# A third buffer for raw weight blocks, v loaded two to three units later into three buffers, and seven buffers for split factors

## The chip, the cores and the metric

The kernel runs on one core of a Trainium2 chip. The metric is the device time of one execution in microseconds. The profile is of one further execution; its times are in us from the start of its span.

## What is computed

Three stages follow one another: a local attention over chunks of 32 queries, a first gated layer (w1, w2, w3 and w_out of `moe`), and a second gated layer (w_a, w_b and w_out of `moe2`).

```python
# attention: q, k, v (4, 8, 768, 64), 8 memory rows; chunk 32, 16 to the left, 8 to the right
scores = scale * q_c @ concat(mem_k, k_ctx).T          # per chunk and head
a = exp(scores - max); a = a / (sum(a) + 1e-9)
out = a @ concat(mem_v, v_ctx)
# first layer, x (3072, 512)
x = ((x @ w1) * (x @ w2) @ w3) @ w_out                  # d_ff 1024
# second layer
y = ((x @ w_a) * (x @ w_b)) @ w_out                     # d_ff 1536
```

## The kernel before

The kernel works in float32. A factor of a product is split into a high and a low part in one narrower form, and three matrix multiplies replace one. The weights arrive as 64-bit words, in **raw blocks** of 128 x 512 x 8 bytes (512 KB). A raw block is scaled by two ScalarE instructions in place (`w_scale`, L358 and L359) and put together by three VectorE instructions (`w_bits`, L363 to L365); in what follows these three are "the sum" of the block. After the sum its buffer is free.

**Stage 0** multiplies w3 by w_out (the tiles `wps`, the loop from L562) in two halves of 8 steps k with 4 products m each. **The first layer** (`ti` from 0 to 5, 512 tokens each) makes `psA`, `psB` and `psY`, in 24 half-steps of a dozen multiplies for each `ti`. **The second layer** (from the last `ti` on) uses seven products in place of eight per pair of blocks; its factors are made from w_a and w_b by `c_weights` during the first layer, split into `co` tiles (L139, L142) and stored to DRAM (L470).

The engines run their instructions in the order in which the program issues them, and this order is written out by hand. Three streams are woven together in it:

- **Attention.** There are 64 units u (half of the heads of 96 queries). `attn_slot` runs one slot s; a unit takes three slots. The stages of unit u stand at these slots: scores (TensorE) at 3u, max (VectorE) 3u+1, exp (ScalarE) 3u+2, norm (GpSimd, L217) 3u+3, transposition (TensorE, `pt`) 3u+5, copy of `pt` (ScalarE, L229) 3u+6, product with v (TensorE, `xp`) 3u+7 for an odd u, which takes units u-1 and u together, and the split into `xt` at 3u+8. `a_load` loads k, q and v of a unit on the SyncE queue at slot 3u-4 for u up to 23, and at 3u-7 after that. `kbuf` and `qbuf` have two buffers, `vraw` has six. The program loads k, q and v of unit 1 twice.
- **Weights of stage 0 and the first layer.** `plan` is a list of 40 raw blocks, numbered from 0. `w_tick` is one step: the low part of an older block, the high part of another, the sum of block n, the scaling of block n+1, and then as many loads as there are free buffers. Blocks up to 25 take buffers from two pools in turn (`BUFS["raw64"]` gives their number: 2 in `stage`, 3 in `p0`), later ones from `stage` alone. So a load waits on SyncE for the sum that freed its buffer, and what the program issues on SyncE after it waits too.
- **Weights of the second layer.** `blocks_of` loads the 24 raw blocks of w_a and w_b with the two buffers of `stage`, one load after each sum, two blocks ahead.

Within a slot the program issues the stages first (x, pv, pt, trans, norm, exp, max, scores), then the loads. In stage 0, first half, each k issues one tick and a slot after m = 1, and one tick and two slots after m = 3. In the second half, k below 6, one slot follows m = 1, and one or two ticks and then one or two slots follow m = 3. In the first layer each half-step issues a tick (later one step of `c_weights`) and then one or two slots.

In the last `ti` the attention's pool is closed and `co` moves from two buffers in `stage` to a pool of its own (`cop`, 8 buffers).

Of the kernel before, what the change touches and what calls it, by code (L numbers as in the profile page):

```python
# [7 lines left out]
F32 = mybir.dt.float32  # L8
F32R = mybir.dt.float32r
U32 = mybir.dt.uint32  # L10
# [3 lines left out]
P = 128  # L14
B, H, S, D = 4, 8, 768, 64
# [5 lines left out]
HH = 4  # L21
TT = 512
NT1 = B * S // TT
NU = B * NG * 2
# [6 lines left out]
M2 = DF2 // P  # L31
NEG = -1.0e30
CH = 512
BUFS = {"raw64": (2, 3), "dec": (2, 4)}
W3FB = 8
A0 = (1, 2)
TB = 2
# [7 lines left out]
def tile_attention_moe(  # L45
# [24 lines left out]
    stage = stagestack.enter_context(tc.tile_pool(name="stage", bufs=2))  # L70
# [3 lines left out]
    att = astack.enter_context(tc.tile_pool(name="att", bufs=2, side="right"))  # L74
# [32 lines left out]
    vraw, masked = {}, [None, None]  # L107

    def a_mask(u, eng):
        if u < NPLAIN and masked[u % 2] != kind_of(u):  # L110
            masked[u % 2] = kind_of(u)
            m = mask[0:GQ:CHUNK, kind_of(u), :]
            eng.dma_start(
                out=kbuf[u % 2][D:KA], in_=m[:, None, :].to_broadcast([3, HH, KW])
            )
# [9 lines left out]
        eng.dma_start(out=qbuf[u % 2][0:D], in_=qt[u])  # L125

    def a_v(u):
        v = vraw[u] = att.tile([P, HH * D], F32, tag="vraw", bufs=6, name="vraw")
        nc.sync.dma_start(out=v, in_=vw[u])

    def a_load(u):
        if u >= NU:
            return
        a_mask(u, nc.sync)
        a_qk(u, nc.sync)
        a_v(u)

    def split_hi(hi, src):
        nc.scalar.activation(hi, src, AF.Copy)  # L139
# [145 lines left out]
    def attn_slot(n=1):  # L285
        for _ in range(n):
            s = acount[0]
            if s >= NSLOT:
                return
            acount[0] += 1  # L290
            for off, stage_of in STAGES:
                u, r = divmod(s - off, 3)
                if r == 0 and 0 <= u < NU:
                    stage_of(u)

            if s % 3 == 0 and s // 3 + 1 > NPLAIN + 1:
                a_prep_lo(s // 3 + 1)
            if s % 3 == 2 and s // 3 + 2 > NPLAIN + 1:
                a_prep_hi(s // 3 + 2)
            if s % 3 == 0 and NPLAIN <= s // 3 + 1 <= NPLAIN + 1:  # L300
                a_prep_hi(s // 3 + 1)
            if s % 3 == 1 and NPLAIN <= s // 3 + 1 <= NPLAIN + 1:
                a_prep_lo(s // 3 + 1)
            if s % 3 == 2:
                if s // 3 + 2 <= NPLAIN + 1:
                    a_load(s // 3 + 2)
                if s // 3 + 3 >= NPLAIN + 2:
                    a_load(s // 3 + 3)

# [17 lines left out]
    def w_tile(i, tag, shape):  # L329
        x = 0  # L330
        if i < NW0:

            x = int(turn[tag][1] * BUFS[tag][0] < turn[tag][0] * BUFS[tag][1])
        n = BUFS[tag][x]
        if live[tag][x] == n:
# [95 lines left out]

    def blocks_of(stage, src, out, bufs):

        raws = []

        def load():
            if src:
                r = stage.tile([P, CH, 2], U32, tag="raw64", bufs=2, name="raw64")  # L440
                nc.sync.dma_start(out=r.rearrange("p c w -> p (c w)"), in_=src.pop(0))
                raws.append(r)

        load()
        load()
        yield
        while raws:
            r = raws.pop(0)
            w_scale(r)
            yield  # L450
            a = stage.tile([P, CH], U32, tag="dec", bufs=bufs, name="dec")
            w_bits(a, r)
            load()
            out.append(a.bitcast(F32))
            yield

    def c_weights():
        blocks = []
        conv = blocks_of(stage, [wab[f, :, c] for f in range(M2) for c in range(2)], blocks, 2)

        def halves(items):


            n = CH // 2
            x, hl = {}, {}
            for i in range(len(items) + 1):
                if i > 0:
                    co, hi, lo = hl.pop(i - 1)
                    split_lo(lo, x.pop(i - 1), hi)
                    nc.sync.dma_start(out=items[i - 1][0], in_=co.bitcast(F32))  # L470
                for m in range(i, min(i + 2, len(items))):
                    if m not in x:
                        x[m] = items[m][1]()
                if i < len(items):
                    pool, bufs = co_in[0]
                    co = pool.tile([P, 2, n], F32R, tag="co", bufs=bufs, name="co")
                    hi, lo = co[:, 0, :], co[:, 1, :]
                    if len(x[i].shape) == 3:
                        hi, lo = (v.rearrange("p (k f) -> p k f", k=2) for v in (hi, lo))
                    split_hi(hi, x[i])  # L480
                    hl[i] = co, hi, lo
                yield

        def add(x, y, op):
            z = stage.tile([P, CH // 2], F32, tag="cs", bufs=2, name="cs")
            z = z.rearrange("p (k f) -> p k f", k=2)
            nc.vector.tensor_tensor(z, x, y, op)
            return z

        next(conv)  # L490
        yield
        for f in range(M2):
            blocks.clear()
            for _ in range(4):
                next(conv)
                yield
            h = [b.rearrange("p (k j f) -> p k j f", k=2, j=2) for b in blocks]
            a11, a12, a21, a22 = h[0][:, :, 0], h[1][:, :, 0], h[0][:, :, 1], h[1][:, :, 1]
            last = []

            def sums(x, y, op):
                last[:] = [add(x, y, op)]
                return last[0]

            items = (
                (0, lambda: a11),
                (3, lambda: sums(a21, a22, ALU.add)),
                (2, lambda: sums(last[0], a11, ALU.subtract)),
                (5, lambda: sums(a12, last[0], ALU.subtract)),
                (4, lambda: sums(a11, a21, ALU.subtract)),  # L510
                (1, lambda: a12),
                (6, lambda: a22),
            )
            yield from halves(
                [(wcd[f][:, i, :].rearrange("p (l c) -> p l c", l=2), x) for i, x in items]
            )
    co_in = [(stage, 2)]
# [170 lines left out]
    for ti in range(NT1):  # L688
        last = ti == NT1 - 1
        gs = {}  # L690
        attn_slot(NEED[ti] - acount[0])
        if last:
            astack.close()
            tp = ctx.enter_context(tc.tile_pool(name="tp", bufs=2, side="right"))
            costack = ExitStack()
            cop = costack.enter_context(tc.tile_pool(name="cop", bufs=8, side="right"))
            co_in[0] = cop, 8
            xs = []
        for m in range(M1):
            gs[m] = (d1 if m < 4 else d1b).tile(  # L700
                [P, 2, TT], F32R, tag="g2", bufs=4, name="g2"
            )
            ab_step(w12s[m], xt[ti], gs[m], between)
            if last:
                del w12s[m]
                xs.append(x_new())
                if m == 0:
                    w7_load(0)
                if m == 2:
                    b11, b21 = x_first(xs, 0, ti - 1)  # L710
        for n in (0, 2, 1, 3) if last else range(KD):
            psY = psd.tile([P, 512], F32, tag="d", name="psY")
            i = 0
            for m in range(M1):
                for a, b in PASSES:
                    mm(
                        psY[:, :TT],
                        wsm[m][:, a, P * n : P * n + P],
                        gs[m][:, b, :],
                        i == 0,  # L720
                        i == 3 * M1 - 1,
                    )
                    i += 1
                if m == M1 // 2 - 1:
                    between()
            between()
            psY = psY[:, :TT]
            if not last:
                ys = d1b.tile([P, TT], F32, tag="ys", bufs=1, name="ys")
                nc.scalar.activation(ys, psY, AF.Copy)  # L730
                nc.sync.dma_start(out=yd[ti][:, n, :], in_=ys)
            elif n < 2:
                b12 = tmp()
                nc.scalar.activation(b12, psY, AF.Copy)
                t1 = minus(psY, b11)
                x_put(xs[3], n, t1)
            else:
                late = x_rest(xs, n - 2, b11, b21, b12, t1, psY)
                next(late)
                if n == 2:  # L740
                    for _ in late:
                        pass
                    b11, b21 = x_first(xs, 1, ti - 1)
        if last:
            w7_load(1)
# [252 lines left out]
```

## Time and profile before

| | us |
|---|---|
| median of 3 runs | 1143.05 |
| lowest and highest | 1139.79, 1143.15 |
| profiled execution, its own time | 1140.1 |
| its span | 1138.0 |
| TensorE busy in the span | 1096.9 (96%) |
| VectorE busy | 648.3 (57%) |
| ScalarE busy | 516.1 (45%) |
| GpSimd busy | 286.2 (25%) |

A busy share is a mean over stages with different limits, so the reading starts with windows by stage, and goes on to what TensorE waited for in each. The granted clock of TensorE is given as a share of its higher level. An idle time in front of an instruction stands in square brackets with what ended it; a wait for several things is put down to the one that came last.

### The profile page before, as it was taken

To read this page: it belongs to the slowest core of one execution; us is meant where nothing else is said; L and a number is where in the kernel's file an instruction comes from. 1 tells how busy PE (TensorE), PEld (TensorE's weight loads), DVE (VectorE), ACT (ScalarE), POOL (GpSimd) and SP (SyncE) were. 2 spreads that over 40 slices of the span, in tenths; PEclk is the share of its full clock that TensorE was granted. 3 is DMA by queue.
4 is the path that set the end of the run, shared out by engine and by line. 5 is a ranking of instruction groups with operands and counts; after the bars stand their busy time and mean duration, and the time that the engine had idled before them with its cause. 6 is when DMAs were issued, how large, how long until landed. Compare 5 with 4: busy or idle time off the path is not lost.

```text
span 1138.0 us, 15580 instructions
## 1 busy us (share of the span) xinstructions
PE 1096.9 (96%) x5344; PEld 874.6 (77%) x5344; DVE 648.3 (57%) x1374; ACT 516.1 (45%) x1321; POOL 286.2 (25%) x265
## 2 busy tenths in 40 slices
PE   4997999999999999999999999999999999999998
PEld 2554777887777887887887778888888888888887
DVE  6896866787998887874666554343223234232220
ACT  4776664666676575664444434232222223222210
POOL 1111231232232331331203322302323310223210
PEclk9999999999999999999999999999999999999999
DMA  9854435335445334424554554353433451434311
GB/s 268 244 184 127 150 117 182 127 133 172 144 134 179 129 131 167 154 101 149 212 185 185 206 224 152 136 169 107 188 131 132 183 175 60 181 130 177 147 37 37
DMA packets 65684, 174.91 MB, mean 154 GB/s; under 512 B 8168, under 2 KB 20870, under 8 KB 60998
## 3 DMA queue, kind: packets, MB, share of 16 engines
q1 hardware_dynamic: 54791, 107.58, 28.7%
q0 software_dynamic: 10528, 66.08, 15.6%
q8 instruction: 42, 0.69, 0.3%
q14 instruction: 36, 0.29, 0.1%
q10 hardware_dynamic: 287, 0.27, 0.1%
HBM read 140.33 MB, written 33.55 MB: 153 GB/s over the span
## 4 chain that ended last, share of the span: by engine, by line
PE 74%; DVE 4%; ACT 3%; issue 3%; DMA 2%; POOL 1%; SPq 0%; ACTq 0%; DVEq 0%; POOLq 0%
PE ps L784 29%; PE ops L93 17%; PE psA L93 10%; PE psB L93 9%; PE psY L93 6%; DMA wc<-co 1%; PE sc L93 1%; PE xp L93 1%; ACT t L204 1%; PE pt L225 1%; DVE q L142 1%; DVE dec L365 1%; DVE dec L364 1%; POOL t L217 0%; ACT k L139 0%
## 5 line engine op out<-in xcount | busy, mean ns | idle before, releaser
L784 PE MATMUL ps<-x,w 128*128 128x512 f32 x1512 | 349.5, 389 | 3.2 <-ACT tmp L796 3.2
L784 PEld LDWEIGHTS ps<-x,w 128*128 128x128 f32 x1512 | 283.4, 188 | 63.9 <-ACT tmp L796 5.3
L801 DVE TENSOR_TENSOR tmp<-ps,tmp 128x512 f32<-128x512 f32 x108 | 74.6, 691 | 245.3 <-PE ps L784 241.2
L93 PE MATMUL psA<-xt,w 128*128 128x512 f32 x576 | 145.6, 400 | 3.2 <-ACT xt L139 2.3
L93 PE MATMUL psB<-xt,w 128*128 128x512 f32 x576 | 141.0, 393 | 0.0
L93 PE MATMUL psY<-g,wo 128*128 128x512 f32 x576 | 139.0, 393 | 0.0
L217 POOL TENSOR_TENSOR t<-t,sm 96x512 f32<-96x512 f32 x64 | 81.8, 1278 | 222.2 <-DVE sm L216 126.6
L683 POOL DMA_DIRECT2D w<-wc x72 | 39.4, 551 | 368.4 <-PE ps L784 368.0
L796 ACT ACTIVATE tmp<-ps 128x512 f32<-128x512 f32 x108 | 64.4, 596 | 147.3 <-PE ps L784 109.0
L93 PEld LDWEIGHTS psA<-xt,w 128*128 128x128 f32 x576 | 106.3, 190 | 28.1 <-ACT xt L139 3.5
L93 PEld LDWEIGHTS psY<-g,wo 128*128 128x128 f32 x576 | 105.6, 188 | 21.0
L93 PEld LDWEIGHTS psB<-xt,w 128*128 128x128 f32 x576 | 105.5, 188 | 21.0
L93 PE MATMUL ops<-wo,g 128*128 128x512 f32 x504 | 118.6, 389 | 0.0
L618 POOL TENSOR_TENSOR g<-gv,g 128x512 fp32r<-128x512 f32 x48 | 67.8, 1412 | 189.0 <-ACT g L617 170.6
L93 PEld LDWEIGHTS ops<-wo,g 128*128 128x128 f32 x504 | 94.6, 188 | 19.6
L807 ACT ACTIVATE g<-tmp 128x512 fp32r<-128x512 f32 x66 | 40.8, 633 | 130.2 <-DVE tmp L806 130.2
L808 POOL TENSOR_TENSOR g<-tmp,g 128x512 fp32r<-128x512 f32 x66 | 87.4, 1338 | 26.6 <-ACT g L807 25.7
L93 PE MATMUL wps<-wo_f,w3f 128*128 128x512 f32 x128 | 65.0, 640 | 11.1 <-DVE wo_f L365 10.3
L204 ACT ACTIVATE t<-t,mx 96x128 f32<-96x128 f32 x168 | 65.1, 390 | 13.7 <-DVE mx L189 13.6
L93 PE MATMUL ops<-fo,g 128*128 128x512 f32 x288 | 68.2, 389 | 0.0
L358 ACT ACTIVATE raw<-raw 128x512 f32<-128x512 f32 x76 | 50.9, 670 | 30.5 <-DMA raw<-in_w 18.8
L93 PEld LDWEIGHTS ops<-fo,g 128*128 128x128 f32 x288 | 54.1, 188 | 11.2
(79 smaller groups left out, 1276.0 us busy)
## 6 DMA issues: line engine op xcount, KB each, us to landing
w<-wc POOLq DMA_DIRECT2D x36, 1024.0 KB, 6.6
w<-wc POOLq DMA_DIRECT2D x36, 768.0 KB, 4.7
wc<-co SPq DMA_DIRECT2D x84, 256.0 KB, 2.4
raw<-in_wab SPq DMA_DIRECT2D x24, 512.0 KB, 3.8
kraw<-in_kt SPq DMA_DIRECT2D x42, 256.0 KB, 3.0
vraw<-in_vw SPq DMA_DIRECT2D x65, 128.0 KB, 2.9
raw<-in_w3a SPq DMA_DIRECT2D x16, 512.0 KB, 5.1
raw<-in_w SPq DMA_DIRECT2D x16, 512.0 KB, 3.8
```

Of the source, the lines that this page charges most:

```text
L93: nc.tensor.matmul(o, lhsT=l, rhs=r, start=first, stop=last)
L142: nc.vector.tensor_tensor(lo, src, hi.bitcast(F32), ALU.subtract)
L204: nc.scalar.activation(t[:, h, :], src[:, h, :], AF.Exp, bias=mx[:, h : h + 1], scale=scale, accum_out=sm[:, h : h + 1],)
L217: nc.gpsimd.tensor_tensor(t, t, sm[:, :, None].to_broadcast([GQ, HH, KW]), ALU.mult)
L358: nc.scalar.activation(h, h, AF.Copy, scale=2.0**-112)
L618: nc.gpsimd.tensor_tensor(g2[:, 1, :], gv, g2[:, 0, :].bitcast(F32), ALU.subtract)
L683: nc.gpsimd.dma_start(out=t[:, c0:c1].bitcast(F32), in_=src[:, c0:c1])
L784: nc.tensor.matmul(ps, lhsT=w[:, i, a, k, :], rhs=xs[i][:, b, k, :], start=first and n == 0, stop=n == 5, skip_group_check=not first,)
L796: nc.scalar.activation(z, ps, AF.Copy)
L801: nc.vector.tensor_tensor(z, ps, y, ALU.add)
L807: nc.scalar.activation(g2[:, 0, :], z, AF.Copy)
L808: nc.gpsimd.tensor_tensor(g2[:, 1, :], z, g2[:, 0, :].bitcast(F32), ALU.subtract)
```

## The change

The pool `stage` gets three buffers for raw blocks, for `w_load` and for `blocks_of` in `c_weights` alike. `a_load` no longer loads v; instead a slot s with s mod 3 = 1 and s from 10 on loads v of unit s/3 - 1, that is v of unit u at slot 3u+4, into one of three buffers. `cop` has seven buffers in place of eight.

```diff
-BUFS = {"raw64": (2, 3), "dec": (2, 4)}
+BUFS = {"raw64": (3, 3), "dec": (2, 4)}
     def a_v(u):
-        v = vraw[u] = att.tile([P, HH * D], F32, tag="vraw", bufs=6, name="vraw")
+        if u >= NU:
+            return
+        v = vraw[u] = att.tile([P, HH * D], F32, tag="vraw", bufs=3, name="vraw")
         nc.sync.dma_start(out=v, in_=vw[u])
     def a_load(u):
...
         a_qk(u, nc.sync)
-        a_v(u)
     def attn_slot(n=1):
...
                     a_load(s // 3 + 3)
+            if s % 3 == 1 and s // 3 > 2:
+                a_v(s // 3 - 1)
-    def blocks_of(stage, src, out, bufs):
+    def blocks_of(stage, src, out, bufs, raws_n=2):
...
-                r = stage.tile([P, CH, 2], U32, tag="raw64", bufs=2, name="raw64")
+                r = stage.tile([P, CH, 2], U32, tag="raw64", bufs=raws_n, name="raw64")
     def c_weights():
-        conv = blocks_of(stage, [...], blocks, 2)
+        conv = blocks_of(stage, [...], blocks, 2, 3)
...
-            cop = costack.enter_context(tc.tile_pool(name="cop", bufs=8, side="right"))
-            co_in[0] = cop, 8
+            cop = costack.enter_context(tc.tile_pool(name="cop", bufs=7, side="right"))
+            co_in[0] = cop, 7
```

## Rows read from the trace of the kernel before

**Rows 1.** Windows: length; busy PE, PEld, DVE, ACT, POOL; PEclk; DMA share, GB/s.

```profile
0.00:26.00 26.00, 10.47 (x33) 5.26 (x34) 15.17 (x29) 13.56 (x27) 4.15 (x10) 0.95 0.91 274
26.00:84.00 58.00, 56.18 (x280) 31.12 (x281) 53.54 (x108) 43.78 (x137) 10.81 (x10) 0.96 0.72 211
84.00:108.50 24.50, 18.68 (x81) 9.44 (x76) 14.50 (x28) 12.85 (x36) 2.07 (x2) 0.93 0.51 158
108.50:165.00 56.50, 51.07 (x285) 41.44 (x286) 44.54 (x79) 36.78 (x102) 15.55 (x12) 0.97 0.40 126
...
205.00:599.00 394.00, 390.46 (x2121) 317.60 (x2120) 306.96 (x792) 237.53 (x698) 112.29 (x85) 1.00 0.45 152
```

**Rows 2.** Waits of PE from 84 to 166: us in total, times, longest.

```profile
PE xp L93 <- ACT p L229: 4.3, 2, 2.7
PE pt L225 <- ACT raw L358: 3.1, 1, 3.1
PE pt L225 <- POOL t L217: 2.4, 1, 2.4
```

**Rows 3.** Waits of ACT from 84 to 166.

```profile
ACT raw L358 <- DMA raw<-in_w: 15.4, 10, 2.5
```

**Rows 4.** Timeline of PE from 94: start, us, instructions, [idle before <- releaser].

```profile
94.81 0.68 PE L225 MATMUL pt<-id_sb,t 96*128 96x96 f32 x4 [3.13 <-ACT raw L358]
95.28 3.52 PE L93 MATMUL wps<-wo_f,w3f 128*128 128x512 f32 x4
...
99.51 1.88 PE L93 MATMUL wps<-wo_f,w3f 128*128 128x512 f32 x4
...
103.48 0.55 PE L93 MATMUL xp<-p,vraw 128*64 128x96 f32 x8 [1.61 <-ACT p L229]
...
115.56 2.89 PE L93 MATMUL psA<-xt,w 128*128 128x512 f32 x12
...
125.67 0.80 PE L93 MATMUL xp<-p,vraw 128*64 128x96 f32 x8 [2.73 <-ACT p L229]
...
126.40 4.33 PE L93 MATMUL psA<-xt,w 128*128 128x512 f32 x12
```

**Rows 5.** Timeline of VectorE and ScalarE before the stop at 94.81.

```profile
87.74 0.69 DVE L365 CUSTOM_DVE_ANT_0 dec<-raw,dec 128x1024 uint16<-128x1024 uint16 x1
...
89.90 0.67 ACT L358 ACTIVATE raw<-raw 128x512 f32<-128x512 f32 x1 [2.40 <-DMA raw<-in_w]
```

**Rows 6.** Timeline around the load of k of unit 10.

```profile
69.38 0.47 SPq L124 DMA_DIRECT2D kraw<-in_kt  x1
...
71.97 0.69 DVE L365 CUSTOM_DVE_ANT_0 w3f<-raw,w3f 128x1024 uint16<-128x1024 uint16 x1
...
75.46 1.04 PE L93 MATMUL sc<-kraw,qraw 67*96 67x128 f32 x8
```

**Rows 7.** Timeline around the product with v of units 2 and 3.

```profile
44.50 0.33 SPq L346 DMA_DIRECT2D raw<-in_w3b  x1
44.92 0.47 SPq L124 DMA_DIRECT2D kraw<-in_kt  x1
...
47.96 1.01 PE L93 MATMUL xp<-p,vraw 128*64 128x96 f32 x16
```

**Rows 8.** DMA issues of the whole span: count, KB each, median us to landing.

```profile
vraw<-in_vw SPq DMA_DIRECT2D x65, 128.0 KB, 2.9
...
qraw<-in_qt SPq DMA_DIRECT2D x64, 96.0 KB, 3.9
...
raw<-in_w3b SPq DMA_DIRECT2D x8, 512.0 KB, 4.5
```

**Rows 9.** Timeline of PE: two further waits in stage 0.

```profile
62.00 1.98 PE L93 MATMUL wps<-wo_f,w3f 128*128 128x512 f32 x4 [0.71 <-DVE wo L558]
...
69.76 1.08 PE L93 MATMUL sc<-kraw,qraw 67*96 67x128 f32 x8 [0.80 <-DMA qraw<-in_qt]
```

**Rows 10.** Waits of the SyncE queue: us in total, times, longest.

```profile
SPq L441 <- DVE dec L365: 201.1, 28, 12.5
```

**Rows 11.** Timeline of VectorE beside a GpSimd instruction.

```profile
118.23 1.67 DVE L364 SCALAR_TENSOR_TENSOR dec<-raw,dec 128x512 uint32<-128x512 uint32 x1
```

More of the change, by code (lines that the diff above doesn't have):

```diff
@@ L458, in c_weights @@
         blocks = []
-        conv = blocks_of(stage, [wab[f, :, c] for f in range(M2) for c in range(2)], blocks, 2)
+        conv = blocks_of(stage, [wab[f, :, c] for f in range(M2) for c in range(2)], blocks, 2, 3)
         def halves(items):
```

## Prediction

> **What bounds the kernel now.** I read the windows by stage first. From 205 us to 599 us TensorE is busy 390.46 of 394 us, and the second layer behind it holds only products that the change does not touch, so what can be won or lost lies before 205 us [rows 1]. Three stages differ there. Up to 26 us the DMA engines are 91% busy and TensorE waits for weights. From 26 to 84 us TensorE (56.18 of 58) and VectorE (53.54 of 58) are both nearly full. From 84 to 165 us TensorE is busy 18.68 of 24.5 and 51.07 of 56.5 us: some 11 us are idle, and VectorE has 10 and 12 us to spare [rows 1].
>
> Then the waits of TensorE between 84 and 166 us: 3.1 us once for `pt`, put down to a scaling of a raw block, 4.3 us in two stops for the copy of `pt` that ScalarE makes, and 2.4 us for the norm on GpSimd [rows 2]. What ScalarE itself waits for in the same stretch is ten times a raw block, 15.4 us in all [rows 3]. So TensorE is stopped by exp and copies that stand behind a scaling on ScalarE, and the scaling stands behind a load. The timeline shows why: the sum of a block ends at 88.43 (87.74 + 0.69), only then is its buffer free for another load, while the next scaling already waits for a load of the tick before and starts at 89.90 after 2.40 us of idle time [rows 5]. A w3b block takes 4.5 us from issue to landing in the median [rows 8].
>
> The stops cost more than their length. After the one at 94.81 four multiplies took 3.52 us, and 1.88 us a little later; after the one at 125.67 twelve took 4.33 us against 2.89 before [rows 4]. That is the lower of TensorE's two levels (1.2 against 2.4 GHz, the factor of 1.87) for a while: 1.64 and 1.44 us.
>
> **The change part by part.** The order of the work on TensorE, ScalarE, VectorE and GpSimd is the same; the DMAs move along SyncE and one v load (unit 1, loaded twice) goes. The sum is made against the profiled execution, 1140.1 us, which lies 0.26% below the median of 1143.05.
>
> *Raw blocks, 84 to 165 us.* From block 27 on each load has two ticks to land instead of one. The wait of ScalarE before 94.81 goes. I follow its chain: with 2.40 us out of ScalarE, exp and norm end about 92 us, when TensorE has just finished its multiplies (94.81 less 3.13 is 91.68), so the whole stop and its slow clock go: 3.13 + 1.64 = **4.8 us** (3.1 if the clock falls anyway). At 103.48 the copy of `pt` stands behind a scaling too, but also behind a high part that needs a VectorE sum; I take 0.9 of the 1.61 us (0 to 1.6). At 125.67 the two scalings ahead waited by 1.5 us each in the mean (15.4 / 10), and a high part between them needs VectorE's sum; I take 2.0 of 2.73 us, and the 1.44 us of clock with it: **3.4 us** (1.2 to 4.2). The 2.4 us for the norm come through VectorE, which is late by the same waits; half of it, 1.2 (0 to 2.4).
>
> *Raw blocks, k behind them.* This part costs. SyncE issues in order, so what stands behind a load waits for the sum that this load waits for. Going through the ticks by hand: k of unit 10 stood behind a load that reuses the buffer of block 20; with three buffers a load that reuses the buffer of block 22 comes just ahead of it. That sum ends at 72.66 (71.97 + 0.69), VectorE is 92% busy in this stage [rows 1] and won't be earlier, and k was issued at 69.38 [rows 6]. So k goes out at about 73.1 and q at 73.6, and q lands 3.9 us later [rows 8], at 77.4; the scores started at 75.46 [rows 6]. Cost 1.9 us (0.1 with half of that landing, 4 with one and a half). Against it, TensorE's later waits for q of 0.80 us and its kind run down: unit 12's load has no raw load ahead of it any more. I give back 0.9 and take **+1.0** (0 to +4).
>
> *v later.* For an odd unit u the load stands at slot 3u+4, behind the raw load of the same tick, and TensorE uses it at 3u+7. For unit 3 that place is where k of unit 6 stood: 44.92, behind a raw block issued at 44.50 [rows 7]. The block lands 4.5 us later [rows 8], at 49.0, and v 0.5 us after it (128 KB at the 274 GB/s of the full stretch [rows 1]); TensorE wants it at 47.96 [rows 7]. A stop of 1.5 us. A v load by itself takes 2.9 us [rows 8], and the margin is 3.0, so the block ahead of it decides. Within the next 22 us TensorE waits 0.71 and 0.80 us for other things that a later TensorE would not wait for [rows 9], so this is given back: **0** (0 to +2). For units 7, 9 and 11 the v load stands right behind the q load without a sum before it; from unit 17 on SyncE is more than a slot ahead of TensorE. The wait for a free v buffer is for a product three slots back, less tight than the one that k has for its scores two slots back.
>
> The Trainium skill (DMA: Bandwidth & Descriptors, Anatomy of one DMA) fits a transfer as 2.0 us plus its bytes at 436 GB/s, for another issue path. By it, as an estimate, q would take 2.2 us and v 2.3, q of unit 10 would cost 0.4 and v of unit 3 nothing, and the sum below would be -10.8; the trace's medians of 3.9 and 2.9 us [rows 8] decide here.
>
> *The start.* One v load less (128 KB) before the sixth block, but a sixth block (512 KB) ahead of k of unit 2, in a stretch where the DMA engines are full: 384 KB at 274 GB/s are 1.4 us for k, against 0.6 us won for the sixth block. Net **0** (-1 to +1).
>
> *Raw blocks of w_a and w_b.* SyncE waited 201.1 us for sums before these loads, 28 times [rows 10]; nothing of it reaches TensorE, which has 3.5 us of gaps in 394 [rows 1]. 0 (-1 to +1). *Seven `co` buffers:* a buffer comes back after seven halves, some 10 us at two halves per half-step of 2.9 us [rows 4], and its store is half the size of a raw block, which lands in 4.5 [rows 8]. 0; if that cover were gone, ScalarE would wait once per half.
>
> Sum: -4.8 - 0.9 - 3.4 - 1.2 + 1.0 = **-9.3 us**. Against the profiled execution 1130.8, against the median **1133.8**. The bounds together reach from -15 to +4.
>
> **The rivals.** *All of ScalarE's waiting comes back* and k costs nothing: 4.8 + 1.6 + 4.2 + 2.4 = 13.0, time 1130.0. For it speaks that VectorE has 22 us to spare after 84 us; against it the sums in between.
>
> *VectorE is the bound.* It has 92% in 26 to 84 us [rows 1], and work that runs closer together meets GpSimd more often: beside GpSimd an instruction of the sum took 1.67 us, alone 0.69 [rows 11, 5]. Then only the stop at 94.81 goes (-4.8), k costs its 1.0, and one or two more such meetings 1.0 each: -2.3, time 1140.7. The Trainium skill (SBUF — State Buffer, Who interferes with whom) says that a VectorE instruction with two inputs in SBUF and a GpSimd instruction that reads SBUF share a port; the 1.67 us agree.
>
> *Slower: SyncE's order becomes the new bound.* Loads of k and v reach the queue too late at units 3, 5, 10, 13 and 15. Price: unit 10 at its bound 4.0 and the slow clock after it 1.6; the four v loads 1.5 each; of the gains 4.8 and 1.2 stay. 11.6 - 6.0 = +5.6, time 1148.7. It decides from where v lands later than 3.0 us after its turn (47.96 - 44.92) at each of these units. Against it: after 60 us the DMA engines are no longer full, so the raw block ahead lands sooner.
>
> *The loads don't start earlier,* because SyncE is held by k's wait for scores and gets to the raw loads no sooner: 0, time 1143.05.
>
> **How the numbers follow.** Forecast 0.50, all comes back 0.12, VectorE 0.20, slower 0.13, nothing 0.05. The range of 1129 to 1143 takes in all but the slower case and the tails. About 0.3%, 3.4 us, is what a measurement can tell from no change. Faster by more: 0.48 of the forecast, 0.12, and 0.06 of VectorE's case, 0.66. Within: 0.21. Slower: 0.13.
>
> **What would show it.** ScalarE's waits for raw blocks after 84 us, 15.4 us before, should be under 3; the stops at 94.81 and 125.67 gone, without a fall of the granted clock. A new wait of TensorE for q at unit 10 near 75 us and for v near 48 us, of 1 to 3 us each. If TensorE's waits from 84 to 166 us stay as long but are put down to VectorE, the second rival holds. If waits of `xp` for v appear at many units, I am wrong.

## The result and the profile after

| | before | after |
|---|---|---|
| median, us | 1143.10 (4 runs) | 1130.39 (4 runs) |
| lowest and highest, us | 1139.79, 1143.95 | 1128.85, 1134.21 |
| ratio, 95% interval | | 0.9892 [0.9872, 0.9911] |
| profiled execution, span, us | 1140.1, 1138.0 | 1134.21, 1132.1 |

The change saves 12.7 us by the medians. The forecast was 9.3 us less, 1133.8, with a range of 1129 to 1143. The sum came out near, but terms of it were wrong in opposite directions, and the experiments are about these.

The windows by stage of the changed kernel have the columns of [rows 1]; the stretch from 165 to 205 us is new.

```profile
0.00:26.00 26.00, 10.74 (x32) 5.31 (x32) 14.38 (x29) 12.80 (x26) 3.63 (x10) 0.97 0.91 280
26.00:84.00 58.00, 53.00 (x248) 29.70 (x249) 52.26 (x103) 43.99 (x136) 10.32 (x10) 0.91 0.74 218
84.00:108.50 24.50, 23.68 (x112) 12.63 (x111) 16.95 (x36) 14.72 (x44) 3.12 (x3) 0.96 0.45 135
108.50:165.00 56.50, 53.45 (x300) 43.54 (x299) 46.59 (x79) 37.45 (x107) 17.07 (x13) 0.97 0.41 135
165.00:205.00 40.00, 39.87 (x222) 32.51 (x221) 25.90 (x72) 22.67 (x73) 8.96 (x7) 1.00 0.52 167
205.00:599.00 394.00, 389.87 (x2117) 316.88 (x2116) 306.62 (x786) 238.50 (x696) 114.19 (x88) 1.00 0.46 152
```

From 84 to 108.5 us TensorE is busy 23.68 us where it was 18.68, from 108.5 to 165 us 53.45 where it was 51.07. The stage ahead of them got worse: 53.00 where it was 56.18, with the granted clock at 0.91 where it was 0.96. The waits of TensorE from 84 to 166 us answer [rows 2]:

```profile
PE pt L226 <- POOL t L218: 2.0, 1, 2.0
PE xp L93 <- DMA vraw<-in_vw: 0.6, 1, 0.6
PE psA L93 <- ACT xt L140: 0.5, 1, 0.5
PE xp L93 <- ACT p L230: 0.4, 1, 0.4
PE psA L93 <- DVE xt L143: 0.2, 1, 0.2
```

The stop for `pt` of 3.1 us is gone, and the two for its copy have shrunk from 4.3 us to one of 0.4; the norm's stop has stayed (2.0 of 2.4). ScalarE's waits in that stretch had raw blocks at their head, 15.4 us [rows 3]. Now a raw block is not among them; what leads is its own work for the gate:

```profile
ACT g L620 <- DVE gv L619: 11.8, 6, 2.8
ACT w L396 <- DVE dec L368: 6.5, 4, 2.4
```

The timeline of TensorE in the changed kernel: the two new stops, what followed the second, and the places of the old ones [rows 4].

```profile
50.98 0.55 PE L93 MATMUL xp<-p,vraw 128*64 128x96 f32 x8 [1.30 <-DMA vraw<-in_vw]
...
78.95 1.99 PE L93 MATMUL sc<-kraw,qraw 67*96 67x128 f32 x8 [2.04 <-DVE w3f L368]
80.74 6.10 PE L93 MATMUL wps<-wo_f,w3f 128*128 128x512 f32 x8
...
96.98 0.49 PE L226 MATMUL pt<-id_sb,t 96*128 96x96 f32 x4
...
122.20 0.55 PE L93 MATMUL xp<-p,vraw 128*64 128x96 f32 x8 [0.41 <-ACT p L230]
```

The stop at 78.95 is put down to a VectorE instruction of a sum, which ended at 78.90. The scores don't need it: in a second profile of the same kernel (below) they start at 79.35, before the same instruction ends (79.67), and there the wait, of 1.86 us, is put down to q. The SyncE queue of the first profile shows why q is late:

```profile
69.99 4.08 SPq L349 DMA_DIRECT2D raw<-in_w  x2
74.16 0.47 SPq L124 DMA_DIRECT2D kraw<-in_kt  x1
74.69 0.59 SPq L125 DMA_DIRECT2D qraw<-in_qt  x1
```

Two raw loads go out, the second only when the sum has ended at 73.7; k and q of unit 10 stand behind it, k at 74.16 where it was 69.38 [rows 6], and the scores start 4.3 us after q went out at 74.69. That is the chain the prediction traced by hand: k at 73.1, q at 73.6, a landing of 3.9 us.

To place the time I took the start of the same TensorE instruction in both traces, at seven points, and list how far the changed kernel is ahead (negative) or behind after each stretch. The second profile of the changed kernel is from a later run on another chip (span 1129.2 us). The stretches are named by the times of before; the last column has the terms of the forecast, put where they should have shown.

| stretch | first profile | second profile | forecast |
|---|---|---|---|
| start to 58.5 | +2.4 | +2.3 | +1.5 (v of unit 3) |
| 58.5 to 81.6 | +3.9 | +2.5 | +0.4 (q of unit 10, less 1.5 given back) |
| 81.6 to 108.5 | -7.4 | -7.4 | -6.6 |
| 108.5 to 141.2 | -3.9 | -3.9 | -3.4 |
| 141.2 to 171.6 | +1.9 | +0.4 | -1.2 (norm) |
| 171.6 to 201.4 | -2.4 | -2.4 | 0 |
| 201.4 to the end | -0.4 | -0.4 | 0 |
| sum | -5.9 | -8.8 | -9.3 |

The first row is not the stop for v alone: 1.2 and 1.9 us of it are there at 44 us, ahead of the place of that stop, and a kernel below that has no such stop (raw loads behind k, q and v, second run) is 3.1 us behind there. So a difference of 1 or 2 us in the stretches up to 58.5 us lies within what two executions differ by.

The second profile is the typical one (its execution took 1131.36, the median beside it was 1131.06), the first is the longest of its four. The profile of before, 1140.1, lies 3.7 to 4.1 us under the medians of before in two of the sets below (1143.78 and 1144.20); the third gave 1142.72. That is why 8.8 us between two profiles are 12.7 between medians.

### The profile page after: what moved, and what is told of

The parts are those of the page before. It is cut to its first block, busy times and chain, and to the rows that moved or that the text cites. A ratio compares the mean times of both kernels' runs of the same rounds, so it can differ in the third digit from the quotient of the medians.

```text
span 1132.1 us, 15601 instructions
## 1 busy us (share of the span) xinstructions
PE 1098.0 (97%) x5344; PEld 876.0 (77%) x5344; DVE 647.7 (57%) x1374; ACT 516.5 (46%) x1321; POOL 286.1 (25%) x265
## 4 chain that ended last, share of the span: by engine, by line
PE 81%; DVE 3%; issue 2%; ACT 2%; DMA 1%; POOL 1%; DVEq 0%; ACTq 0%; POOLq 0%; SPq 0%
PE ps L787 29%; PE ops L93 17%; PE psA L93 11%; PE psB L93 10%; PE psY L93 10%; PE sc L93 2%; PE xp L93 2%; PE pt L226 1%; ACT t L205 1%; POOL t L218 0%; DVE dec L367 0%; DMA wc<-co 0%; DVE dec L368 0%; DMA vraw<-in_vw 0%; DVE xt L143 0%
## 5 line engine op out<-in xcount | busy, mean ns | idle before, releaser
L218 POOL TENSOR_TENSOR t<-t,sm 96x512 f32<-96x512 f32 x64 | 81.6, 1275 | 214.5 <-DVE sm L217 116.9
L620 ACT ACTIVATE g<-gv 128x512 fp32r<-128x512 f32 x48 | 30.2, 629 | 71.4 <-DVE gv L619 71.4
```

Of the source, the lines that this page charges most:

```text
L218: nc.gpsimd.tensor_tensor(t, t, sm[:, :, None].to_broadcast([GQ, HH, KW]), ALU.mult)
L620: nc.scalar.activation(g2[:, 0, :], gv, AF.Copy)
```

## Experiments

My theory was that of the prediction: the third buffer in stage 0 and the first layer carries the gain, the later v costs nothing in the end, and the raw blocks of w_a and w_b and the seven `co` buffers change nothing. The rival: the gain and the cost lie elsewhere, in SyncE's order, where a load of k, q or v stands behind a raw load that waits for a sum. In every kernel below the order of the work on TensorE, VectorE, ScalarE and GpSimd is the same; only SyncE's order, the number of buffers and the waits differ.

### v later, alone

The kernel before, with `a_v` as in the change; two raw buffers, eight `co` buffers.

```diff
-        v = vraw[u] = att.tile([P, HH * D], F32, tag="vraw", bufs=6, name="vraw")
+        v = vraw[u] = att.tile([P, HH * D], F32, tag="vraw", bufs=3, name="vraw")
...
-        a_v(u)
...
+            if s % 3 == 1 and s // 3 > 2:
+                a_v(s // 3 - 1)
```

> The kernel before with the v part alone: v loaded at slot 3u+4 into three buffers, raw blocks and co as before. My theory (v gives nothing, it only makes room): the stop at the product with v of unit 3 is there, about 1.3 us, the ScalarE waits for raw blocks of 15.4 us after 84 us stay, and the time is 0 to 2 us above before, ratio 1.000 to 1.002. Rival (the lighter DMA traffic of the start is the gain): 4 us or more below before, ratio under 0.9965.

Measured: 1147.07 us (10 runs) beside 1143.78, ratio 1.0032 [1.0015, 1.0048]. It costs 3.3 us, so the expectation of 0 to 2 us missed, and the rival, a gain, fell. The trace of this kernel, SyncE first, then TensorE:

```profile
44.52 0.33 SPq L349 DMA_DIRECT2D raw<-in_w3b  x1
44.95 0.38 SPq L131 DMA_DIRECT2D vraw<-in_vw  x1
...
50.90 0.55 PE L93 MATMUL xp<-p,vraw 128*64 128x96 f32 x8 [2.27 <-DMA vraw<-in_vw]
...
52.08 3.24 PE L93 MATMUL wps<-wo_f,w3f 128*128 128x512 f32 x4
...
207.41 2.02 PE L93 MATMUL psA<-xt,w 128*128 128x512 f32 x4 [1.32 <-ACT xt L140]
```

v is issued right behind a raw block that waited for a sum, at the place that the prediction named (44.92). It goes out 3.1 us ahead of the product (which starts at 48.08 with unit 2), and unit 3's part of the product can start only 5.9 us after that, at 50.9. The four multiplies behind the stop take 3.24 us, at TensorE's lower level for most of them (the profile of before has 2.06 here). A second stop stands at 207.41, where the second block of 512 tokens begins. The first is given back in part: against the profile of before the kernel loses 3.9 us from 44 to 54 us and wins 2.0 back by 70 us, where the waits of [rows 9] are gone. At the second it loses 1.5 us from 201 to 281 us. Its lag at the end, 8.4 us, can't be read as a cost: the kernel with seven `co` buffers, which measures as before, is 7.4 us behind the same profile.

The second kernel moves v ahead of one such wait: the same, with the raw loads issued after k, q and v of the slots that follow a tick.

```diff
+        w_loads()                      # end of attn_slot
...
-        while w_load():                # end of w_tick
-            pass
+    def w_loads():
+        while w_load():
+            pass
...
             nplan[0] += w_tick()
+            if acount[0] <= 0 or not wraw:
+                w_loads()
```

> The v part alone, as in the run with v late, but with the raw loads issued on SyncE behind the v, k and q loads of the slots after a tick. The v part alone cost 3.3 us with a stop of 2.3 us for v of unit 3. My theory (the raw block ahead of it on SyncE makes v late, not the three buffers nor the later slot): the stop is gone and the time is at most 1 us above before, ratio 0.998 to 1.001. Rival (three buffers are too few, or the slot is too late): the stop stays, ratio 1.002 to 1.005.

Measured: 1144.60 (10 runs) beside 1144.20, ratio 1.0009 [0.9991, 1.0027]. v of unit 3 goes out at 43.03, ahead of the raw block of that tick (though behind the one before it), 5.9 us before its product, and the stop is gone. The second stop stays:

```profile
43.03 0.38 SPq L131 DMA_DIRECT2D vraw<-in_vw  x1
...
48.93 1.02 PE L93 MATMUL xp<-p,vraw 128*64 128x96 f32 x16
...
207.65 4.76 PE L93 MATMUL psA<-xt,w 128*128 128x512 f32 x12 [1.62 <-ACT xt L140]
```

With two buffers ScalarE waits for raw blocks as before (the same view as [rows 3]):

```profile
ACT raw L362 <- DMA raw<-in_w: 17.0, 11, 2.7
```

So, as far as the ratios go, most of what v later costs alone comes with the wait ahead of it. But the two intervals overlap by 0.12%, and the edit moves k and q ahead of the raw blocks too, so that their share isn't separated.

### The third buffer, one half at a time

Both have the changed kernel's v and `co`. The first gives the third buffer to w_a and w_b alone (`w_load` keeps two), the second to `w_load` alone (w_a and w_b keep two); in both the third buffer has its own tag, `raw64c`.

```diff
-BUFS = {"raw64": (3, 3), "dec": (2, 4)}
+BUFS = {"raw64": (2, 3), "dec": (2, 4)}
```

> The changed kernel, but the loads for stage 0 and the first layer use two stage buffers again (the third one has a tag of its own and serves only the blocks of w_a and w_b). My theory: the gain is gone, ScalarE waits for raw blocks are back at 13 to 17 us after 84 us, the scores of unit 10 no longer stop, ratio 1.000 to 1.002 against before. Rival (SyncE's 201 us of waiting for sums before the w_a and w_b blocks were the cost): ratio stays at 0.989 to 0.993.

```diff
-        conv = blocks_of(stage, [...], blocks, 2, 3)
+        conv = blocks_of(stage, [...], blocks, 2, 2)
```

> The mirror of the run before: the third stage buffer serves only the loads for stage 0 and the first layer, the blocks of w_a and w_b use two. My theory: the whole gain, ratio 0.988 to 0.992, ScalarE waits for raw blocks after 84 us under 1 us. Rival (w_a and w_b): 0.998 to 1.002.

Measured beside 1143.78: 1140.70 (10 runs), ratio 0.9969 [0.9950, 0.9988], for w_a and w_b alone; 1136.72 (4 runs), ratio 0.9934 [0.9911, 0.9956], for stage 0 and the first layer alone. Against v later alone (1147.07) these are -6.4 and -10.4 us. The intervals leave some 3 us on either difference. The three add up within that: +3.3 - 6.4 - 10.4 = -13.5, and the whole change gave -12.7 and, in a second set, -13.1. Both expectations missed, each with its rival: the gain is neither all in stage 0 and the first layer nor all in w_a and w_b, whose blocks have a good third of what the third buffer wins against v later alone.

The trace of before, between 176 and 188 us (SyncE, ScalarE, TensorE), shows where:

```profile
176.19 0.33 SPq L441 DMA_DIRECT2D raw<-in_wab  x1
176.62 0.38 SPq L124 DMA_DIRECT2D kraw<-in_kt  x1
...
180.89 0.63 ACT L139 ACTIVATE k<-kraw 128x512 fp32r<-128x512 f32 x1 [4.76 <-DMA kraw<-in_kt]
...
185.43 0.42 ACT L139 ACTIVATE co<-cs 128x256 fp32r<-128x256 f32 x1 [2.70 <-DMA wc<-co]
...
187.65 0.71 PE L93 MATMUL sc<-k,q 128*96 128x256 f32 x4 [2.19 <-ACT t L204]
```

A w_a/w_b load waits for a sum until 176.19; k stands behind it; ScalarE, which splits k in order, is idle for 4.76 us, and for 2.70 more in front of a `co` buffer whose store was issued after k; exp stands behind both, and the next scores wait 2.19 us for exp. The changed kernel has no stop here: TensorE is busy 39.87 of the 40 us from 165 to 205, where it was busy 37.68, and the same scores run without a wait:

```profile
182.17 0.68 PE L93 MATMUL sc<-k,q 128*96 128x256 f32 x4
```

The wait of ScalarE for a `co` buffer is there as before (2.75 us at 178.36), but k is split ahead of it, at 172.95. The kernel gains 2.4 us in this stretch in both of its profiles (table above). SyncE's waits before w_a/w_b loads, 201.1 us [rows 10], fell to:

```profile
SPq L444 <- DVE dec L368: 110.7, 16, 13.2
```

The two half kernels say the same. With the third buffer for w_a and w_b alone, the scores run without a wait; with it for `w_load` alone they stop as before:

```profile
191.97 0.69 PE L93 MATMUL sc<-k,q 128*96 128x256 f32 x4
```

```profile
181.85 1.17 PE L93 MATMUL sc<-k,q 128*96 128x256 f32 x4 [2.31 <-ACT t L205]
```

The stop at 207 that v later had added is gone in both. So part of the 6.4 us repairs what v later broke: 2.4 us are the old stop, 1.5 the new one. The other 2.5 us have no place in the traces, and the 1.5 are in the 10.4 us of the other half too, so the sum above counts them twice.

### k, q and v ahead of the raw loads

The changed kernel, with the raw loads behind k, q and v (the diff of the second kernel above, on the changed kernel). It ran twice, the second time beside the changed kernel itself.

> The changed kernel, with the loads of raw blocks issued on SyncE behind the k, q and v loads of the slots that follow a tick instead of ahead of them. The order on the four computing engines is the same. My theory (k of unit 10 stands behind the sum of block 22, v of unit 3 behind a raw block): the stops of 2.0 us near 79 and 1.3 us near 51 go, and with the first the slow clock after it; time 2 to 5 us below the changed kernel, ratio to before 0.984 to 0.988. Rival (these stops are hidden behind VectorE, which is 90% busy there): same as the changed kernel, 0.988 to 0.991. Other rival (raw blocks a little later bring ScalarE's waits back): above the changed kernel.

> The changed kernel once more, on the same chip as the next run, as its measure. [...]

> The changed kernel with raw loads behind k, q and v on SyncE, once more. My theory: 2 to 5 us below the changed kernel on the same chip, ratio to before 0.984 to 0.987, mean granted clock 0.997 or higher in most runs. Rival: the difference to the changed kernel seen before was the chip's, and both come out within 1 us.

Measured: 1128.99 (4 runs) beside 1143.78, ratio 0.9865 [0.9844, 0.9887]; then 1129.15 (4 runs), ratio 0.9862 [0.9841, 0.9883], where the changed kernel gave 1131.06 (4 runs), ratio 0.9885 [0.9868, 0.9901], beside 1144.20. In the second run's trace k and q of unit 10 go out ahead of the two raw loads, and the waits of TensorE up to 84 us hold neither q nor v:

```profile
69.87 0.47 SPq L124 DMA_DIRECT2D kraw<-in_kt  x1
70.40 0.59 SPq L125 DMA_DIRECT2D qraw<-in_qt  x1
71.93 4.09 SPq L350 DMA_DIRECT2D raw<-in_w  x2
...
PE wps L93 <- DVE wo_f L369: 10.3, 1, 10.3
PE pt L226 <- POOL t L218: 5.4, 2, 4.6
PE wps L93 <- DVE wo L566: 0.7, 1, 0.7
```

Neither stop is in the trace of the first run. That the stop for q came from the raw loads in front is shown. That taking the stops away is worth 1.9 us is not: it has that sign against both sets of the changed kernel (0.9865 and 0.9862 against 0.9892 and 0.9885), but the intervals overlap, and the expected clock of 0.997 or more in most of its runs was met by one of four (0.995 to 0.997, where the changed kernel showed 0.997 to 0.998 beside it). It is the fastest version of this study.

### v one slot earlier

The changed kernel with v of unit u at slot 3u+3, raw loads in their old place.

```diff
-            if s % 3 == 1 and s // 3 > 2:
+            if s % 3 == 0 and s // 3 > 2:
```

> The changed kernel with v of unit u loaded at slot 3u+3 instead of 3u+4, the raw loads in their old place. If v is late because a raw block of the same tick stands ahead of it on SyncE, v of unit 3 goes out ahead of the block, TensorE has no stop for v near 51 us, and the time is 1 to 3 us below the changed kernel's (0.986 to 0.988 of the kernel before); q of unit 10 is still late by 2 us near 79 us, which the kernel with all raw loads behind does not show. If v is late because a slot is too little time whatever stands ahead of it, the stop at 51 us shrinks but stays (0.5 us or more), and the time is that of the changed kernel (0.988 to 0.990).

Measured: 1132.89 (6 runs) beside 1142.72, ratio 0.9909 [0.9891, 0.9926]. The stop went as the first theory has it, and the time didn't follow. v goes out 2.4 us ahead of the block of its old slot, 6.0 us before its product, and unit 3 has no stop (compare 50.98 above); the late q of unit 10 stays. Another block stands right ahead of v, at 42.27, so the run doesn't tell that block's share from the mere time:

```profile
42.27 0.33 SPq L349 DMA_DIRECT2D raw<-in_w3b  x1
42.69 0.38 SPq L131 DMA_DIRECT2D vraw<-in_vw  x1
45.12 0.33 SPq L349 DMA_DIRECT2D raw<-in_w3b  x1
...
48.71 0.89 PE L93 MATMUL xp<-p,vraw 128*64 128x96 f32 x16
...
78.21 1.16 PE L93 MATMUL sc<-kraw,qraw 67*96 67x128 f32 x8 [1.94 <-DMA qraw<-in_qt]
79.16 5.26 PE L93 MATMUL wps<-wo_f,w3f 128*128 128x512 f32 x8
```

In this trace the kernel is 1.9 us ahead of the changed one's second profile at 49 us (1.2 of it ahead of the stop's place, at 44) and 0.9 ahead at 134 us, and by 166 us it is 0.7 behind: the norm's stop took 2.6 us in place of 1.7, and the granted clock from 108.5 to 165 us was 0.97 in place of 1.00. So with three raw buffers the stop for v is worth nothing that a measurement shows; with two, v later cost 3.3 us. Part of the difference is the stop at 207, which no kernel with a third buffer has; the rest was not separated.

### The `co` buffers

Three instead of seven in the changed kernel, and seven instead of eight in the kernel before.

```diff
-            cop = costack.enter_context(tc.tile_pool(name="cop", bufs=7, side="right"))
-            co_in[0] = cop, 7
+            cop = costack.enter_context(tc.tile_pool(name="cop", bufs=3, side="right"))
+            co_in[0] = cop, 3
```

> The changed kernel with three buffers for split factors in the last part of the first layer in place of seven. My theory (a store lands in 2.4 us, three halves take over 4 us, so even three cover it): as the changed kernel, ratio to before 0.988 to 0.991, no new wait of TensorE. Rival (the cover was thin and seven had already cost something): ScalarE waits for stores of co by 5 us or more longer, and 1 to 4 us above the changed kernel.

> The kernel before with seven co buffers instead of eight and nothing else. If seven still cover the stores (ScalarE waited 8.5 us for a co buffer from 500 to 640 us with eight, 8.0 us with seven, and 23.8 with three): 0.998 to 1.002 of the kernel before, ScalarE's waits for a co buffer between 8 and 10 us. If each buffer less costs a part of the 8.9 us that three cost (four steps from seven to three, some 2.2 us each): 1.002, and ScalarE's waits for a co buffer above 11 us.

Measured with three: 1139.95 (4 runs) beside 1144.20, ratio 0.9958 [0.9942, 0.9974], 8.9 us above the changed kernel on the same chip; the expectation was wrong. With seven in the kernel before: 1144.68 (12 runs) beside 1142.72, ratio 1.0006 [0.9993, 1.0020]; the first of its two theories. ScalarE's waits for a `co` buffer from 500 to 640 us, in turn with three, with seven (the changed kernel, second profile) and with seven in the kernel before:

```profile
ACT co L140 <- DMA wc<-co: 23.8, 10, 5.1
```

```profile
ACT co L140 <- DMA wc<-co: 8.0, 3, 2.8
```

```profile
ACT co L139 <- DMA wc<-co: 9.0, 3, 4.0
```

With eight it was 8.5 us, in three waits. So the eighth buffer bought nothing that shows, but the cover was never the one that I described: ScalarE waits for a store even with eight. With three buffers the kernel is 8.6 us ahead of before at 525 us in its trace and has lost all of it by the end. Eight `co` buffers beside the third raw buffer, and v in six buffers beside it, were not tried.

## Why the forecast was near, point by point

**The stop at 94.81.** Right. The whole stop and the low clock after it went: the same place, at 96.98, has no wait. The stretch from 81.6 to 108.5 us won 7.4 us in both profiles, where -4.8, -0.9 and the 0.9 given back make -6.6.

**The stops at 103.48 and 125.67.** Right, and a little small: 2.73 us became 0.41, and the stretch from 108.5 to 141.2 us won 3.9 us against 3.4. ScalarE's waits for raw blocks were to fall under 3 us; none is left.

**The norm.** The step that failed is "half of it": the stop stayed, 2.0 us in the first profile and 1.7 in the second, after a stop of 0.6 and 1.0 for v of unit 15 near 140 us. In the three traces of changed kernels without that stop it is 2.6. I had put half of it down to a VectorE that is late for want of raw blocks. Those came early, and GpSimd ended just as late: in both traces the norm starts right behind GpSimd's multiply for the gate, which waited for ScalarE's `g` (that multiply at 154.38 and the norm at 155.61 before, 149.72 and 150.96 after). In the first profile twelve multiplies behind the stop took 4.43 us, where the profile of before has 3.01; with the stop for v this makes the 1.9 us in the table.

**k of unit 10.** The chain was right to a microsecond (k at 74.16 for 73.1, a stop of 2.0 us for 1.9). The term was too small for what surrounds the stop: from 70 to 81.6 us the two profiles lose 4.9 and 2.9 us. In the first the clock fell behind the stop and took another 2.5 us, which the sum left out (it stood only in a rival, at 1.6). In the second, q of unit 11 stopped TensorE too, by 1.3 us (at 85.53) where before has 0.3. The Trainium skill (DMA: Bandwidth & Descriptors, Anatomy of one DMA) fits a DMA on GpSimd's path as 2.0 us plus its bytes at 436 GB/s; by it, as an estimate, q would land in 2.2 us. Here, on SyncE's queue and behind two raw blocks, the scores start 4.3 and 3.9 us after q's issue, so the measurement decides.

**v later.** In the changed kernel the term of 0 held, and for the stated reason. The stop is at the named place, 1.3 us in the first profile and 0.5 in the second for 1.5:

```profile
50.92 0.55 PE L93 MATMUL xp<-p,vraw 128*64 128x96 f32 x8 [0.46 <-DMA vraw<-in_vw]
```

From 44 to 54 us the two lose 1.2 and 0.4 us against before, and from 58.5 to 70 us they win 1.1 and 0.4 back, where the two waits of [rows 9] (1.5 us together) have shrunk to 0.6 and 1.0. The stop for v of unit 15 comes back at the norm (2.0 and 0.6, or 1.7 and 1.0, for 2.4). The kernel with v a slot earlier bears this out. The landing is less steady than the medians say: TensorE starts 5.0 (45.95 to 50.98), 4.2 and, with v late alone, 5.9 us after the issue of v, where I had put 4.6; a v issued 5.9 to 6.0 us ahead of its product stopped nothing in three kernels. On its own the part cost 3.3 us, and what an argument by unit 3 alone misses there is the low clock behind a stop of 2.3 us and a second stop far from it, at 207 us.

**The raw blocks of w_a and w_b.** The step that failed is "nothing of it reaches TensorE": priced at 0, worth 2.4 us of visible stop against before, and 6.4 us (with some 3 us of uncertainty) in the kernel with v late. The reason I gave rests on the stretch from 205 us on [rows 1]; but these loads begin before that, and the one stop that they cause, 2.19 us at 187.65, lies between my windows, which skipped from 165 to 205 us. The 201.1 us [rows 10] were read as slack of a queue; what counts is who stands behind a wait there, and at 176 us it was k.

**Start.** The bound held: at 26 us the two profiles are 0.8 us behind and 0.2 us ahead. (128 KB at the 274 GB/s used there are 0.5 us, not 0.6.) **Seven `co` buffers.** The value held (ratio 1.0006), the reason didn't, as told above.

**The rivals.** *VectorE is the bound* fell: it is busy 16.95 of 24.5 us in the stage that gained most, and TensorE waits for it 0.2 us from 84 to 166. (The 0.69 us in [rows 5] is L365's; L364, which took 1.67 beside GpSimd, takes 0.69 alone as well, its median in the trace.) *SyncE's order* was half true: its stops came at unit 3, at unit 10, at unit 15 with 0.6 and 1.0 us, and once at unit 11, but not at units 5 and 13, and the gains were far larger. *All comes back* gives the median within 0.4 us (1130.0) by the wrong way: the norm stayed and k did cost.

**The sum.** Against the profile that I worked from, -9.3 stood for -8.8: misses of +2.9 (up to 81.6 us), +1.6 (norm and unit 15) and -4.1 (the rest, 2.4 of it the blocks of w_a and w_b) cancel but for 0.5. That the total came so near is luck in part. The remaining 4 us of the 12.7 lie between the profiled execution of before and its medians. Executions of before differ by 8 us, and the longer ones show less clock: of 19 on one chip, the six at a mean granted clock of 0.991 took 1146.1 in the median, the five at 0.994 took 1141.7. The changed kernel stood at 0.997 to 0.998 in its second set. The clock isn't all: the profile of before showed 0.993, and others at 0.993 took 1142.7.

Traces show where a longer execution loses it. Four kernels whose `w_load` has two raw buffers were profiled in executions 1.1 to 3.0 us above their medians: v late, v late with the raw loads behind, the third buffer for w_a and w_b alone, and seven `co` buffers, which is the program of before up to its last `ti`. All four are 1.2 to 2.6 us slower than the profile of before from 81.6 to 108.5 us. The stop at 103.48 [rows 4] is 2.0 to 3.5 us there, and the eight multiplies behind it take 4.9 to 6.4 us, where the profile of before has 3.70. With seven `co` buffers:

```profile
105.10 0.91 PE L93 MATMUL xp<-p,vraw 128*64 128x96 f32 x8 [3.53 <-ACT p L229]
105.93 6.39 PE L93 MATMUL wps<-wo_f,w3f 128*128 128x512 f32 x8
```

No kernel with the third buffer in `w_load` loses clock here. So the 0.9 us for this stop, read from one short execution, was too little for the usual one, and part of the 4 us lies here; how much, no run separates.

## What to carry to other kernels

Where loads for several users go out on one in-order queue, read each wait of that queue by who stands behind it, not by its total; a load that waits for a buffer belongs behind the loads that wait for nothing (here that took two stops away and cost nothing that shows). Lay the windows over the whole span without a gap, since a stop in a stretch that no window covers is priced at nothing. Price a new stop with and without a fall of the clock, and look for a second one behind it. Compare traces stretch by stretch, and against more than one execution: a single profile can be a short one just where the gain is to be read.

## What the runs showed of the hardware

The same stop can cost its length or more than twice that. In the changed kernel's second profile the stop for q of unit 10 was followed by eight multiplies at the higher level:

```profile
79.35 1.09 PE L93 MATMUL sc<-kraw,qraw 67*96 67x128 f32 x8 [1.86 <-DMA qraw<-in_qt]
80.28 3.60 PE L93 MATMUL wps<-wo_f,w3f 128*128 128x512 f32 x8
```

In the first profile, behind a stop of 2.04 us, the same eight took 6.10 us (above), with a granted clock of 0.59 from 80 to 87 us against 1.00 here: 2.5 us for the same program at the same place. Ahead of it TensorE had done the same work in both. The length of a stop doesn't decide it either: the norm's stop at 157.15 in the profile of before, 2.42 us, was followed by twelve multiplies in 3.01 us, and the same stop with seven `co` buffers, 2.41 us, by twelve in 4.61.

And with less clock a kernel isn't always longer: the fastest version ran at 0.79 from 26 to 50 us in its second run, and was still the shorter one (1127.8 against 1129.2).
